# RetNet attention into a SwiGLU FFN on one core: second weight chunk and first unit's norm and product moved to earlier places

## The chip, the cores and the metric

The kernel runs on one core of one Trainium2 chip. The metric is device time in microseconds (us), from the first to the last instruction of the core, as the median of several executions. The engines are named as in the profile: PE (TensorE, matrix products) with PEld (its weight loads), DVE (VectorE), ACT (ScalarE), POOL (GpSimd) and SP (SyncE, which issues most of the transfers).

## The reference

Eight batches with eight heads of 576 rows by 64: retention (causal attention with a decay for each head in place of a softmax), then an RMS norm and a SwiGLU feed-forward over 4608 rows of 512.

```python
scores = scale * np.matmul(q, k.transpose(0, 1, 3, 2))
ret = scores * Dmat[None]                  # gamma_h ** (i - j) below the diagonal, else 0
attn = np.matmul(ret, v)                   # -> x: (4608, 512)

rms = np.sqrt(np.mean(x * x, axis=-1, keepdims=True) + 1e-06)
xn = x / rms * rms_g
g = xn @ w_gate                            # 512 x 1536
silu = g * (1.0 / (1.0 + np.exp(-g)))
val = xn @ w_val                           # 512 x 1536
out = silu * val @ w_out                   # 1536 x 512
```

q, k and v are float32. The three weight matrices arrive as float64 and must be rounded to float32 on the chip.

## The kernel before

The work is cut in two ways. Attention goes by *jobs*: a pair of heads of one batch. Jobs 0 to 3 are batch 0; jobs 4 to 7 are the first third of batch 1. The feed-forward goes by *units* of 384 rows: unit 0 needs jobs 0 to 3, unit 1 also jobs 4 to 7. This start, in which jobs 0 to 7 run while the first weights are loaded and rounded, is what the change edits. From unit 2 on, the kernel follows a regular pattern that stays as it is.

A job's q and k are turned (transposed) on PE with ACT copying the result out of PSUM, then `slot(j)` does the products of job j and the second half of job j - 1:

```python
def slot(j, rest=True):
    if rest and j > 0:
        values(j - 1)      # PE: av <- ret, v; then a memset of "tick" on POOL behind its last product
    if j < len(jobs):
        scores(j)          # PE: s <- qT, kT
        states(j)          # PE: s <- v, k
    if j < len(jobs):
        weigh(j)           # DVE: ret
    if j < 2 * NHP:
        sums(j)            # DVE: running state
    if rest and j > 0:
        carried(j - 1)     # PE: av <- qT, sum, waits for tick; then DVE: x <- av * gq (L435)
    ...
```

The norm of a unit is in four steps: `square` on ACT and `gather` on DVE (L487), `norm_1` (PE: mean square `ms`, L499; DVE: `r`, L504; POOL: POW, L505), `diagonals` on DVE (L547), and `norm_2` (PE: broadcast `rb`, L562; DVE: four scalings of x, L564).

The products of the first two units are made by a generator that yields after each. Half 0 of a matrix comes before half 1:

```python
def up_plain(u, m, g):
    if not (m or g):
        h_of[u] = ...
    for half in range(2):
        for i in (2 * g, 2 * g + 1):
            ps = bank(f"up_{u}_{m}_{half}_{i}")
            for c in range(NHP):
                nc.tensor.matmul(
                    ps[:, :U], lhsT=w_up[m][:, 4 * half + c, i * P : i * P + P],
                    rhs=x_of[u][:, c], start=(c == 0), stop=(c == NHP - 1),
                )
            h = h_of[u][:, half * NH + i]
            if m:
                nc.vector.tensor_tensor(out=h, in0=h, in1=ps[:, :U], op=ALU.mult)
            else:
                nc.scalar.activation(out=h, in_=ps[:, :U], func=AF.Silu)
            yield
```

The float64 weights come in chunks of 1024 KB. Chunk 0 is half 0 of the first columns of w_gate, chunk 1 is half 1, chunks 2 and 3 are the same of w_val. A chunk's words are read in integer and float steps, each one step of the generator `rounding`; `weights(n)` takes n steps:

```python
exponent(i)   # DVE L874: shift and mask; queues three Relus (L890) that act() gives to ACT later
yield
# mantissa(i):
#   DVE L901: mask; yield
#   DVE L906: add of the low word; yield
#   act(chunk=i): Relus still queued; DVE L911: sign; the room of the words is free
load_chunks(i + 5 if i else 0, nc.sync)
yield
# where chunk i + 1 is loaded: exponent(i + 1); yield
join(i)       # DVE L919: mantissa * exponent -> the float32 weights
yield
```

The start itself, before the change:

```python
load_chunks(1)
...
weights(3)
for j in range(2 * NHP):
    load_first(j, {0: range(2), 1: range(2, H)}.get(j))
    ...
    load_chunks((1, 1, 1, 1, 2, 2, 2, 3)[j], nc.sync)
...
turn(0)
scale_v(0)
act(3)
squares = []
...
for j in range(2 * NHP):
    slot(j)
    if j + 1 < 2 * NHP:
        turn(j + 1)
    if squares:
        gather(*squares.pop())
    for i in ((1,), (2,), (3,), (4, 5), (6,), (7,), (), ())[j]:
        scale_v(i)
    if j:
        u, c = divmod(j - 1, NHP)
        squares.append((u, c, square(u, c)))
    act(1)
    if j == 5:
        norm_1(0)
    elif j == 6:
        norm_2(0)
    weights((2, 0, 0, 1, 1, 1, 1, 0)[j])
    if j == 4:
        gather(*squares.pop())
    elif j == 5:
        diagonals(0)
    act(1)
gather(*squares.pop())
...
now = 0
for m, g in [(m, g) for g in range(NG) for m in range(2)]:
    for u in range(2):
        weights_to(4 * g + 2 * m + 1)
        for i, _ in enumerate(up_plain(u, m, g)):
            later(now)       # jobs 8 to 11 and their loads, at fixed counts
            now += 1
            if not (u or m or g):
                if i == 0:
                    values(2 * NHP - 1)
                    carried(2 * NHP - 1)
                    gather(1, NHP - 1, square(1, NHP - 1))
                elif i == 1:
                    norm_1(1)
                elif i == 2:
                    diagonals(1)
                elif i == 3:
                    norm_2(1)
            weights(2)
            act(1)
            if u and m and g == NG - 1:
                weights_to(len(chunks))
                next(made, None)     # combinations of w_out's blocks, DVE L690
            if i == 1:
                weights_to(4 * g + 2 * m + 2)
```

The order of instructions on each engine is that of the program. After this loop come the products across for units 1 and 0 (L726), which need differences of h (DVE, L710).

Of the kernel before, what the change touches and what calls it, by code (L numbers as in the profile page):

```python
# [41 lines left out]
def kernel(  # L42
# [11 lines left out]
    nc = tc.nc  # L54
# [242 lines left out]
    def scores(j):  # L297


        d = st[j]  # L300
        _, _, c0, c1 = jobs[j]
        s = d["s"] = trio.tile([P, 3, 512], F32, tag="s", name=f"s_{j}")
        for c in range(c0 // 2 * 2, (c1 + 1) // 2 * 2):
            i, odd = divmod(c, 2)
            c = min(max(c, c0), c1 - 1)
            for e in range(2):
                nc.tensor.matmul(  # L307
                    s[side(odd), e, i * L : i * L + L], lhsT=d["kT"][side(e), c * L : c * L + L],
                    rhs=d["qT"][side(e), c * L : c * L + L], start=True, stop=True,
                )  # L310
# [131 lines left out]
    def slot(j, rest=True):  # L442

        if j > len(jobs):
            return
        if rest and j > 0:
            values(j - 1)
        if j < len(jobs):
            scores(j)
            states(j)  # L450
        if j < len(jobs):
            weigh(j)
        if j < 2 * NHP:
            sums(j)
        if rest and j > 0:
            carried(j - 1)
        if 2 * NHP <= j < len(jobs):
            sums(j)
# [36 lines left out]
    def norm_1(u):  # L495

        ms = bank(f"ms_{u}")
        for s in range(NS):
            nc.tensor.matmul(  # L499
                ms[:, s : s + 1], lhsT=t_of[u][:, s * P : s * P + P], rhs=mean_w,  # L500
                start=True, stop=True,
            )
        r = tmp.tile([P, NS], F32, tag="r", name=f"r_{u}", bufs=1)
        nc.vector.tensor_scalar(out=r, in0=ms[:, :NS], scalar1=EPS, scalar2=None, op0=ALU.add)  # L504
        nc.gpsimd.tensor_tensor(out=r, in0=r, in1=mhalf.to_broadcast([P, NS]), op=ALU.pow)  # L505
        t_of[u] = r
# [45 lines left out]
    def norm_2(u):  # L552

        x = x_of[u]
        g = rms_k
        rb = t_of[u]
        if u < 3:
            g = rms_g  # L560
            rb = bank(f"rb_{u}")[:, :U]
            nc.tensor.matmul(rb, lhsT=ones, rhs=t_of[u], start=True, stop=True)  # L562
        for c in range(NHP):
            nc.vector.scalar_tensor_tensor(  # L564
                out=x[:, c], in0=x[:, c], scalar=g[:, c : c + 1], in1=rb,
                op0=ALU.mult, op1=ALU.mult,
            )
        if u < 2:
            return
        b11, b12 = x[:, :2, :HU], x[:, :2, HU:]  # L570
        b21, b22 = x[:, 2:, :HU], x[:, 2:, HU:]
        t = ffn.tile([P, 3, 2, HU], F32, tag="sums", name=f"sums_{u}")
        t2, t3, t4 = (t[:, i] for i in range(3))
        for o, a, b in ((t3, b22, b12), (b12, b12, b11), (t2, b22, b12), (t4, b21, t2)):
            nc.vector.tensor_tensor(out=o, in0=a, in1=b, op=ALU.subtract)

        t_of[u] = b11, b21, b12, t4, t2, t3, b22
# [282 lines left out]
    def load_chunks(n, queue=nc.scalar):  # L860

        nonlocal n_loads
        while n_loads < min(n, len(chunks)) and waits_at.get(spare(n_loads)) is None:
            load_chunk(n_loads, queue)
            n_loads += 1
# [96 lines left out]
    def weights(n):  # L962

        for _ in range(n):
            next(steps, None)
# [11 lines left out]
    def start():  # L977

        nonlocal now
        h_of[0] = ffn.tile([P, NF, U], F32, tag="h", name="h_0")  # L980
        tables = list(zip((causal, gv, gc, gq, gx), (_causal_table(), *_decay_tables(H, D))))

        def table(i, queue):
            t, values_ = tables[i]
            src = nc.inline_tensor(values_, name=t.tensor.name + "_table")
            queue.dma_start(out=t, in_=src.ap())

        make_identity(nc, ident)
        nc.scalar.activation(out=tick, in_=mhalf[:1], func=AF.Silu)
        nc.vector.memset(ones, 1.0)  # L990
        warm = bank("warm")
        for _ in range(6):
            nc.tensor.matmul(warm[:, :P], lhsT=ones, rhs=ones, start=True, stop=True)
        first_places.update(find_places())
        load_chunks(1)
        for i in (1, 0, 2):
            table(i, nc.scalar)
        weights(3)
        for j in range(2 * NHP):
            load_first(j, {0: range(2), 1: range(2, H)}.get(j))  # L1000
            if j == 1:
                table(3, nc.sync)
            load_chunks((1, 1, 1, 1, 2, 2, 2, 3)[j], nc.sync)
        table(4, nc.sync)
        nc.sync.dma_start(out=rms_g, in_=moe_rms_g.rearrange("(c p) -> p c", p=P))
        load_chunks(4, nc.sync)
        turn(0)
        scale_v(0)
        act(3)
        squares = []  # L1010

        def later(step):

            for i, at in enumerate((LATER_AT[0] - 9,) + LATER_AT[:-2]):
                if step == at + 2:
                    prepare_next(2 * NHP - 1 + i)
                elif step == at + 3:
                    load_next(2 * NHP - 1 + i)
            if step in LATER_AT:
                j = 2 * NHP + LATER_AT.index(step)  # L1020
                if j < LATER_JOBS:
                    slot(j, rest=(j > 2 * NHP))
                else:
                    values(j - 1)
                    carried(j - 1)

        for j in range(2 * NHP):
            slot(j)
            if j + 1 < 2 * NHP:
                turn(j + 1)  # L1030
            if squares:
# [4 lines that stand above are left out]
                u, c = divmod(j - 1, NHP)  # L1036
                squares.append((u, c, square(u, c)))
            act(1)
            if j == 5:
                norm_1(0)  # L1040
            elif j == 6:
                norm_2(0)
            weights((2, 0, 0, 1, 1, 1, 1, 0)[j])
            if j == 4:
                gather(*squares.pop())
            elif j == 5:
# [3 lines that stand above are left out]
        load_qk(2 * NHP)  # L1050
        load_kv(2 * NHP)
        made = combine_out()
        now = 0
        for m, g in [(m, g) for g in range(NG) for m in range(2)]:
            for u in range(2):
                weights_to(4 * g + 2 * m + 1)
                for i, _ in enumerate(up_plain(u, m, g)):
                    later(now)
                    now += 1
                    if not (u or m or g):  # L1060
                        if i == 0:
                            values(2 * NHP - 1)
                            carried(2 * NHP - 1)
                            gather(1, NHP - 1, square(1, NHP - 1))
                        elif i == 1:
                            norm_1(1)
                        elif i == 2:
                            diagonals(1)
                        elif i == 3:
                            norm_2(1)  # L1070
# [4 lines that stand above are left out]
                        next(made, None)  # L1075
                    if i == 1:
                        weights_to(4 * g + 2 * m + 2)
        for _ in made:
            pass
        for blk, t in first_blocks.items():  # L1080
            keep(blk, t)
        rest = across(1)
        next(rest)
        following(LATER_JOBS - 1)
        for i, _ in enumerate(rest):
            if i == 1:
                norm_0(2)
                differences(0)
            elif i == 2:
                norm_1(2)  # L1090
                diagonals(2)
            elif i == 4:
                norm_2(2)
        rest = across(0)
        next(rest)
        combine(1)
        slot(LATER_JOBS, rest=False)
        following(LATER_JOBS)
        for _ in rest:
            pass  # L1100
        combine(0)
        slot(LATER_JOBS + 1)
        load_next(LATER_JOBS + 1)
        turns.append(LATER_JOBS + 1)
# [74 lines left out]
```

## Time and profile before

| what | value |
|---|---|
| median of 3 runs | 1136.8 us (1135.39 to 1137.64) |
| profiled execution, span | 1135.3 us |
| PE busy | 1116.6 us (98%) |
| DVE busy | 732.7 us (65%) |
| mean granted clock of TensorE | 0.994 |
| first product of unit 1 (`up`, L652) starts at | 63.94 us |
| largest wait of PE between 20 and 66 us | 2.5 us, at L241 |

How to read it: the page gives the busy time of each engine over the whole span and in 40 equal slices, one digit of tenths to a slice; PEclk is the clock that TensorE was granted. In a line of a timeline stand the start, the length, the engine, the line of the program, the operation, out<-in by the names of the program, the shape and the count; in brackets, how long the engine had been idle before it and what released it. The waits list, for one engine, the total, the number and the longest.

### The profile page before, as it was taken

Reading aid. Unit: us, or ns where it says so; the run is one execution under the profiler, and the core shown is the slowest. Engines: PE = TensorE matmul, PEld = TensorE weight load, DVE = VectorE, ACT = ScalarE, POOL = GpSimd, SP = SyncE. Lnnn points to the kernel's source line nnn. Section 1 sums busy time; section 2 is a strip of 40 time slices with the busy share of each in tenths; the row PEclk is TensorE's granted clock in tenths of the full one; section 3 lists DMA queues with packets and bytes.
Section 4 is the critical chain, followed back from the end, with each engine's and each line's share of the span. In section 5 each row is a group of like instructions: output and inputs, shape, how many; then the busy total and the mean of one; then the engine's idle time right before and its main releaser. Section 6 shows DMA issues by size and latency. Waiting matters only on the chain.

```text
span 1135.3 us, 24783 instructions
## 1 busy us (share of the span) xinstructions
PE 1116.6 (98%) x10454; PEld 1042.3 (92%) x10454; DVE 732.7 (65%) x1452; ACT 258.6 (23%) x508; POOL 40.9 (4%) x68
## 2 busy tenths in 40 slices
PE   7899999999999999999999999999999999999998
PEld 6655567999999999999999999999999999999998
DVE  5788989655775784485677585465676666446352
ACT  5465551011212211211211121121120210120110
POOL 0000000460000000000000000000000000000000
PEclk9899999999999999999999999999999999999999
DMA  8744568336364374063553555315436503303304
GB/s 193 232 134 148 133 156 241 62 64 154 74 141 110 99 168 136 1 129 81 118 127 50 135 145 103 114 51 103 130 75 138 154 7 98 126 1 100 123 1 112
DMA packets 307040, 126.73 MB, mean 112 GB/s; under 512 B 284528, under 2 KB 289904, under 8 KB 306928
## 3 DMA queue, kind: packets, MB, share of 16 engines
q1 hardware_dynamic: 302640, 123.66, 43.2%
q8 instruction: 82, 1.34, 0.5%
q10 hardware_dynamic: 4288, 1.48, 0.5%
q14 instruction: 30, 0.25, 0.1%
HBM read 110.14 MB, written 14.94 MB: 110 GB/s over the span
## 4 chain that ended last, share of the span: by engine, by line
PE 96%; DVE 1%; DMA 1%; issue 1%; ACT 1%; SPq 0%; POOL 0%; POOLq 0%; ACTq 0%
PE x L595 14%; PE w L595 14%; PE z L595 14%; PE up L652 11%; PE xo L726 8%; PE wo L726 8%; PE zo L726 8%; PE y L595 7%; PE yo L726 4%; PE av L390 2%; PE av L412 2%; PE s L307 2%; PE s L329 1%; PE ms L513 1%; DMA first_sums<-in_v_dram 0%
## 5 line engine op out<-in xcount | busy, mean ns | idle before, releaser
L619 ACT COPY m<-x 128x384 f32<-128x384 f32 x60 | 28.7, 479 | 338.1 <-PE x L595 326.8
L726 PE MATMUL xo<-h,w_out 128*128 128x192 f32 x528 | 90.3, 328 | 0.0
L595 PE MATMUL w<-sums,w_val 128*128 128x192 f32 x480 | 88.6, 328 | 0.3
L595 PE MATMUL x<-x,w_gate 128*128 128x192 f32 x480 | 88.8, 328 | 0.0
L595 PE MATMUL x<-x,w_val 128*128 128x192 f32 x480 | 88.8, 328 | 0.0
L595 PE MATMUL w<-sums,w_gate 128*128 128x192 f32 x480 | 87.9, 326 | 0.0
L595 PE MATMUL z<-x,w_gate 128*128 128x192 f32 x480 | 87.8, 326 | 0.0
L595 PE MATMUL z<-x,w_val 128*128 128x192 f32 x480 | 87.8, 326 | 0.0
L726 PEld LDWEIGHTS xo<-h,w_out 128*128 128x128 f32 x528 | 85.9, 190 | 0.6
L726 PE MATMUL wo<-h,w_out 128*128 128x192 f32 x504 | 85.6, 326 | 0.4 <-DVE c_last L774 0.4
L602 DVE TENSOR_TENSOR u<-m,y 128x384 f32<-128x384 f32 x60 | 33.1, 552 | 79.1 <-PE y L595 79.1
L726 PEld LDWEIGHTS wo<-h,w_out 128*128 128x128 f32 x504 | 82.5, 190 | 0.7 <-DVE c_last L774 0.7
L595 PEld LDWEIGHTS w<-sums,w_val 128*128 128x128 f32 x480 | 79.2, 190 | 2.7 <-DVE c L602 2.7
L595 PEld LDWEIGHTS x<-x,w_gate 128*128 128x128 f32 x480 | 79.2, 190 | 0.8 <-issue 0.3
L595 PEld LDWEIGHTS x<-x,w_val 128*128 128x128 f32 x480 | 79.2, 190 | 0.6
L595 PEld LDWEIGHTS z<-x,w_gate 128*128 128x128 f32 x480 | 79.7, 190 | 0.0
L595 PEld LDWEIGHTS z<-x,w_val 128*128 128x128 f32 x480 | 79.7, 190 | 0.0
L595 PEld LDWEIGHTS w<-sums,w_gate 128*128 128x128 f32 x480 | 79.5, 190 | 0.1
L602 DVE TENSOR_TENSOR h<-u,w 128x384 f32<-128x384 f32 x60 | 33.0, 550 | 69.4 <-PE w L595 69.4
L614 ACT ACTIVATE h<-h 128x384 f32<-128x384 f32 x90 | 47.0, 523 | 88.6 <-DVE h L602 88.6
L652 PE MATMUL up<-x,w_gate 128*128 128x384 f32 x192 | 63.8, 489 | 1.7 <-DVE r L504 1.0
L652 PE MATMUL up<-x,w_val 128*128 128x384 f32 x192 | 63.2, 488 | 0.0
(189 smaller groups left out, 1778.0 us busy)
## 6 DMA issues: line engine op xcount, KB each, us to landing
w_out<-w_blocks SPq DMA_DIRECT2D x70, 768.0 KB, 5.0
out_dram<-o SPq DMA_DIRECT2D x364, 24.0 KB, 1.6
qraw<-in_q_dram SPq DMA_DIRECT2D x96, 72.0 KB, 2.6
kraw<-in_k_dram SPq DMA_DIRECT2D x96, 72.0 KB, 2.6
k<-in_k_dram SPq DMA_DIRECT2D x48, 128.0 KB, 2.9
v<-in_v_dram SPq DMA_DIRECT2D x48, 128.0 KB, 3.0
w_out<-in_moe_w_gate_dram SPq DMA_DIRECT2D x5, 1024.0 KB, 5.4
w_out<-in_moe_w_val_dram SPq DMA_DIRECT2D x3, 1024.0 KB, 5.3
```

The source lines that it names most:

```text
L307: nc.tensor.matmul(s[side(odd), e, i * L : i * L + L], lhsT=d["kT"][side(e), c * L : c * L + L], rhs=d["qT"][side(e), c * L : c * L + L], ...
L329: nc.tensor.matmul(o[side(e)], lhsT=d["k"][side(odd), i, e], rhs=d["v"][side(odd), i, e], start=True, stop=True,)
L390: mm = nc.tensor.matmul(av[odd][column(j, odd, e), i * L : i * L + L], lhsT=d["v"][side(odd), i, e] if c < NC - 1 else d["vt"][:, e], rhs= ...
L412: mm = nc.tensor.matmul(av[odd][column(j, odd, e), i * L : i * L + L], lhsT=d["sum"][c - 1][side(e)], rhs=d["qT"][side(e), c * L : c * L + L],
L513: nc.tensor.matmul(s, lhsT=ones, rhs=y, start=True, stop=True)
L595: nc.tensor.matmul(ps[:, i * HU : i * HU + HU], lhsT=w_up[m][:, 2 * blk + c, cut], rhs=t_of[u][blk][:, c], start=(start and i == c == 0), ...
L602: nc.vector.tensor_tensor(out=o, in0=a, in1=pairs_of(ps), op=ALU.add)
L614: nc.scalar.activation(out=o, in_=c, func=AF.Silu)
L619: nc.scalar.copy(out=s1, in_=pairs_of(x_))
L652: nc.tensor.matmul(ps[:, :U], lhsT=w_up[m][:, 4 * half + c, i * P : i * P + P], rhs=x_of[u][:, c], start=(c == 0), stop=(c == NHP - 1),)
L726: nc.tensor.matmul(ps[:, i * HU : i * HU + HU], lhsT=a[:, c, i * P : i * P + P], rhs=rhs[:, c], start=(start and i == c == 0), stop=False, ...
```

## The change

Four things are moved; no operation is added or taken away.

1. The load of chunk 1 is issued after job 3's loads instead of after job 4's.
2. The steps of its rounding move: one step in job 2, two in job 3, one in job 4, and in job 5 the exponent of chunk 2. The join of chunk 1 stays behind the loop over the jobs.
3. `norm_1(0)` and `norm_2(0)` go ahead of the turns of the next job, so that PE meets them before the transposes.
4. The first product of unit 0 is made in job 6, ahead of slot 7. The generator is created early and resumed later, so the loop over products counts one less: the second product is i = 1 of the first round, job 7's values come after it, and `norm_1(1)` comes after the third product.

What it is for: to give PE work in the waits of the start, and to have the weights and the norm ready sooner.

```diff
-            load_chunks((1, 1, 1, 1, 2, 2, 2, 3)[j], nc.sync)
+            load_chunks((1, 1, 1, 2, 2, 2, 2, 3)[j], nc.sync)
...
         squares = []
+        first = up_plain(0, 0, 0)
...
             slot(j)
+            if j == 5:
+                norm_1(0)
+            elif j == 6:
+                norm_2(0)
             if j + 1 < 2 * NHP:
                 turn(j + 1)
...
             act(1)
-            if j == 5:
-                norm_1(0)
-            elif j == 6:
-                norm_2(0)
-            weights((2, 0, 0, 1, 1, 1, 1, 0)[j])
+            if j == 6:
+                next(first)
+            weights((2, 0, 1, 2, 1, 1, 0, 0)[j])
...
                 weights_to(4 * g + 2 * m + 1)
-                for i, _ in enumerate(up_plain(u, m, g)):
+                whole = u or m or g
+                for i, _ in enumerate(up_plain(u, m, g) if whole else first, 0 if whole else 1):
                     later(now)
                     now += 1
                     if not (u or m or g):
-                        if i == 0:
+                        if i == 1:
                             values(2 * NHP - 1)
                             carried(2 * NHP - 1)
                             gather(1, NHP - 1, square(1, NHP - 1))
-                        elif i == 1:
+                        elif i == 2:
                             norm_1(1)
-                        elif i == 2:
                             diagonals(1)
                         elif i == 3:
                             norm_2(1)
```

## The prediction

> **What bounds the kernel now.** I read the page first, then the chain of waits, then the timelines of the engines up to 70 us. The page:
>
> ```profile
> PE 1116.6 (98%) x10454; PEld 1042.3 (92%) x10454; DVE 732.7 (65%) x1452; ACT 258.6 (23%) x508; POOL 40.9 (4%) x68
> ...
> PE   7899999999999999999999999999999999999998
> PEclk9899999999999999999999999999999999999999
> ```
>
> TensorE (PE) is the bound: after the first two of 40 slices (28 us each) every slice but the last is 9. The change edits the first 65 us, so its worth is how much earlier or later PE enters the saturated part. Everything after follows rigidly. The marker is the first product of unit 1, at 63.94 us before. The waits of PE up to 66 us say what can be won:
>
> ```profile
> PE turn_k L241 <- issue: 2.5, 1, 2.5
> ...
> PE av L390 <- ACT qT L252: 1.2, 2, 0.8
> PE up L652 <- DVE r L504: 1.0, 1, 1.0
> ...
> PE av L412 <- POOL tick L401: 0.8, 2, 0.5
> PE up L652 <- DVE x L564: 0.7, 1, 0.7
> ```
>
> Columns: total us, times, longest. After job 4's transposes begin, the waits are 2.5 (nothing visible released it), 0.8, 0.5, 0.3, 1.0 and 0.7. They sum to 5.8 us, 0.5% of the time: no outcome can leave the 2% band. The timeline of PE at the end of this part:
>
> ```profile
> 51.63 0.45 PE L390 MATMUL av<-ret,h 64*64 64x64 f32 x12
> 52.35 0.45 PE L412 MATMUL av<-qT,sum 64*64 64x64 f32 x8 [0.28 <-POOL tick L401]
> 52.73 2.85 PE L652 MATMUL up<-x,w_gate 128*128 128x384 f32 x8
> 55.41 0.77 PE L499 MATMUL ms<-mean_w,sq 128*128 128x1 f32 x6
> 57.19 5.40 PE L652 MATMUL up<-x,w_gate 128*128 128x384 f32 x16 [1.00 <-DVE r L504]
> 62.42 0.81 PE L562 MATMUL rb<-diag,ones 128*128 128x384 f32 x2
> 63.94 10.59 PE L652 MATMUL up<-x,w_gate 128*128 128x384 f32 x32 [0.71 <-DVE x L564]
> ```
>
> And VectorE (DVE) in the same stretch:
>
> ```profile
> 53.74 0.41 DVE L435 TENSOR_TENSOR x<-av,gq 128x128 f32<-128x128 f32 x2
> 54.74 0.56 DVE L487 TENSOR_TENSOR sq<-sq,sq 128x384 f32<-128x384 f32 x1 [0.59 <-ACT sq L477]
> 55.22 0.68 DVE L874 TENSOR_SCALAR w_gate<-w_out 128x1024 uint32<-128x1024 uint32 x1
> 55.82 1.22 DVE L919 SCALAR_TENSOR_TENSOR w_gate<-w_gate 128x1024 f32<-128x1024 f32 x1
> 56.96 0.15 DVE L504 TENSOR_SCALAR r<-ms 128x3 f32<-128x3 f32 x1
> ```
>
> The 1.0 us at 57.19 is put down to r, but the third product (half 1 of w_gate) needs chunk 1, whose last step is the join at L919, done at 57.04. That join stands in VectorE's program behind job 7's x (L435), the square on ScalarE and the gather (L487).
>
> **What the Trainium skill says.** "TensorE: Matmul & The Clock Gate", Architectural detail: ScalarE and VectorE are strict FIFO, only TensorE reorders, and only weight loads. The trace agrees: the join waits its turn although its inputs were ready long before (sign step at 49.96). Same page, Part 1: the clock is gated by activity in a free-running window of about 3.4 us, half rate after an idle one. The stretches show the granted clock at 0.50 from 33.9 to 37.2 (after the 2.5 us wait) and from 44.2 to 47.4, 1.00 between. "Runtime: NRT & Kernel Launch", Instruction fetch mechanics: instructions come in 16 KiB blocks of 256, the next fetched by a DMA while the current one runs. The page counts 82 packets and 1.34 MB on q8, 16 KB each. The DMA view has one of them starting at 31.0 us, the 2.5 us wait ends at 33.65 between two transposes without a semaphore between them: an instruction fetch, late because chunk 1 (1024 KB, issued 25.73, landed 5.4 us later) lay on the same DMA engines. "DMA: Bandwidth & Descriptors", Queues, rings and completion order: an engine takes a whole packet of one ring before it switches, which fits a delayed and not a blocked fetch.
>
> **The change, part by part** (times in the old kernel's clock; the phase before 22 us doesn't change).
>
> *Chunk 1's load* is issued near 22.1 instead of 25.73. Its contention moves from the fetch at 31.0 to the one that started at 24.36. In the three gaps before, a fetch was usable about 1.5 us after its packet's end (32.11 to 33.65). If the earlier one starts 2 us later, at 26.4, it ends at 27.3 and is usable at 28.8; PE crosses to that block at 27.93, so it waits about 0.9 us there. The next block is asked for then, and needs about 1.3 + 1.0 + 1.5 = 3.8 us uncongested against some 3 us of work in the block: 0.8 more. So 1.7 in place of 2.5 us: **minus 0.8**. But job 3 now has two Relus at its end (2 x 1.15 us on ScalarE) ahead of job 5's copies, and these would then arrive about when they do now: I keep **minus 0.4** of it.
>
> *Rounding sooner.* Exponent, mask and add of chunk 1 (0.68 + 0.68 + 1.22 us) go to jobs 2 and 3, where VectorE waited 1.19 and 1.86 us: mostly hidden. The sign step (1.22) goes to job 4, ahead of the last gather of unit 0, which ends near 40.9 instead of 40.84: nothing. In job 5 the copies of qT no longer queue behind Relus: they waited until 42.37, which was the 0.8 us wait.
>
> *Norm of unit 0 ahead of the turns.* The mean-square product now stands before job 6's turn and needs the gather at 40.9; the old order ran the turn at 40.36. So PE waits 0.5 there, does the ms (0.5) and the turn (1.0), the copies end at 43.0 and job 5's values start at 43.05 instead of 42.78. carried(5) still waits for the POW on GpSimd (44.2), as before: 44.45 against 44.35, **plus 0.1**. The broadcast product runs at 45.1 to 46.35 (half clock), the normalised x is ready from 47.1 to 48.7 instead of 48.4 to 50.0, beside job 7's turn on PE (to 47.9).
>
> *First product ahead of slot 7.* up0 47.9 to 50.5 without the 0.2 it loses now, slot 7 to 51.65, then up1 to 54.25, then values(7) and carried(7) with the tick wait of 0.3: done at 55.4. In the old kernel carried(7) is done at 52.8 with up1 (2.65) still to come: the same work, level to 0.1.
>
> *What follows is the cost.* In the new order nothing stands on PE between carried(7) and the third product, and the join stays behind carried(7) in VectorE's order: x 0.41, square 0.52, gather 0.56, join 1.22 and some 0.2 of hand-overs make 2.9 us. The third product starts near 58.3 instead of 57.19: **plus 1.1**. The ms product of unit 1 (0.55) moves behind it: **plus 0.5**. Its r then comes at 61.6, the POW (1.29) and the diagonals end at 63.8, and now chunk 2's mask and add (0.68 + 1.22) stand between the diagonals and the scaling of x: that starts at 65.6, and unit 1's first product at 66.25, where the old wait would have given 65.4: **plus 0.8**. Without the fetch's minus 0.4 the marker is 66.25 against 63.94, plus 2.3.
>
> *Half clock.* PE idles about 3 us before 58.3. If the window takes that for idle, 3.4 us at half rate follow, of which up to 2.8 hold products: a loss of 1.4 us, at about even odds as the phase is free: **plus 0.7**.
>
> *The end of the first two units.* The count of steps now starts one product later, so job 11's values come after the last up product. VectorE then has x (1.1 us) in front of the last combination (1.75) and the differences (1.35) that the second product across needs. Before, these end at 189.98 and the product starts at 190.19: a slack of 0.2. I get x from 186.4, the differences' end near 190.6: **plus 0.4**.
>
> Sum: 2.3 - 0.4 + 0.7 + 0.4 = 3.0 us. 1136.8 + 3.0 = 1139.8; I shade it to **1139.5** for the gain below.
>
> **Rivals.** (a) The change does what it is for: PE's small waits are filled, and the fetch, freed of chunk 1, comes in time. Then 2.5 us and the half clock after it (1.4) go, and the time could be 1135 or 1134 if the join were not in the way. For it: the fetch is the largest wait. Against: the join's place in VectorE's order, certain from the program. (b) The fetch only moves: all of the 2.5 us stays, now at 27.9, and the half clock with it: 1140. (c) DMA collision: chunk 5 is no longer held until 51.2 but goes at about 40.5, next to chunks 2, 3 and 4, and delays the fetch that started at 43.4. In the new order that block is needed near 50 (48.08 before), so I expect nothing; if it does bite, plus 1 to 2 and 1141. (d) No change to be measured, if gains and costs cancel: 1137.
>
> **Range and chances.** The old runs span 2.2 us. Rival (a) in part gives 1136, everything bad together 1142.8. I take 1136.0 to 1142.8. 2% is 22.7 us, out of reach of all of these: 98% within, 1% each side.
>
> **What would show it.** Right: a wait of 2 to 3 us of PE for VectorE (L919) ahead of the third product, near 55.4 to 58.3; the ms of unit 1 after it; the first product of unit 1 waiting over 1 us for L564, and starting 1.5 to 4 us later than 63.94; up0 near 48 without gaps; a shorter wait at turn_k, with a new one near 28; a short wait of zo for L710 near 190. Wrong: the join before 56, no fetch wait at all, or the marker before 63.9; then the time would be under 1136.

## The result, and the profile after

| | median | range | ratio to before, 95% interval |
|---|---|---|---|
| before | 1136.15 us | 1135.39 to 1137.64 | |
| after | 1147.88 us | 1147.03 to 1149.74 | 1.0104 [1.0086, 1.0121] |

The change makes the kernel 11.7 us slower. The prediction had the sign and one of the causes, but 1139.5 us and a range to 1142.8. The two profiled executions differ by 12.7 us in their spans (1148.0 and 1135.3). The page of the kernel after, of the same two rows as before:

```profile
PE   7889998999999999999999999999999999999998
PEclk9899999999999999999999999999999999999999
```

A slice is 28.7 us. The third (57 to 86 us) and the seventh (172 to 201 us) have an 8 where they had a 9: most of the time is lost in two places, at the start and late in the first two units. The waits of PE from 20 to 260 us (total us, times, longest) name them:

```profile
PE up L652 <- DVE h L658: 3.2, 1, 3.2
PE up L652 <- DVE w_gate L919: 2.9, 1, 2.9
PE ms L499 <- DVE sq L487: 2.0, 1, 2.0
PE av L390 <- issue: 1.2, 1, 1.2
PE up L652 <- DVE x L564: 1.0, 1, 1.0
...
PE turn_k L241 <- issue: 0.6, 1, 0.6
```

Three waits are new. The wait that the prediction took for an instruction fetch (an inference, as no releaser is shown), 2.5 us before, is now 1.2 and 0.6. Where the new ones stand at the start, in the timeline of PE after:

```profile
41.74 1.41 PE L499 MATMUL ms<-mean_w,sq 128*128 128x1 f32 x6 [2.05 <-DVE sq L487]
...
50.20 3.50 PE L652 MATMUL up<-x,w_gate 128*128 128x384 f32 x8
...
54.73 2.85 PE L652 MATMUL up<-x,w_gate 128*128 128x384 f32 x8
...
58.23 0.45 PE L412 MATMUL av<-qT,sum 64*64 64x64 f32 x8 [0.28 <-POOL tick L401]
61.58 4.51 PE L652 MATMUL up<-x,w_gate 128*128 128x384 f32 x8 [2.90 <-DVE w_gate L919]
...
70.94 10.59 PE L652 MATMUL up<-x,w_gate 128*128 128x384 f32 x32 [0.95 <-DVE x L564]
```

The three lines of `up` with 8 records are the first, second and third product (the fourth, at 66.52, is left out), and 70.94 is the marker, the first product of unit 1: 63.94 before, so 7.0 us are lost here. Of these equal products the second takes 2.85 us, the first 3.50 and the third 4.51. The difference is the clock. Stretches of the kernel after (length; busy time of PE, PEld, DVE, ACT, POOL with counts; granted clock; DMA share; GB/s):

```profile
37.90:41.30 3.40, 1.61 (x48) 1.22 (x47) 3.33 (x11) 1.74 (x6) 0.09 (x1) 1.00 0.87 263
41.40:51.50 10.10, 9.71 (x78) 6.58 (x79) 6.76 (x24) 4.27 (x10) 1.32 (x2) 0.50 0.79 296
...
61.90:65.10 3.20, 3.20 (x6) 1.66 (x5) 0.26 (x1) 1.15 (x1) 0.00 (x0) 0.50 0.06 14
...
184.70:188.00 3.30, 3.30 (x7) 1.79 (x6) 3.21 (x9) 0.68 (x2) 0.00 (x0) 0.50 0.88 224
```

The third figure from the right is the granted clock, 1.00 for full speed. Behind each of the three new waits the clock is at half: 10.2 us behind the first, 3.4 behind each of the others. The kernel before had 3.4 us of half clock twice in the same part, at 33.9 and 44.1.

Most of the rest is lost late, from the marker to the first product across (`xo`): 126.9 us after (70.94 to 197.85), 122.35 before (63.94 to 186.29), so 4.6 us more; 1.1 us come behind `xo`. In the kernel after:

```profile
184.21 12.28 PE L652 MATMUL up<-x,w_val 128*128 128x384 f32 x32 [3.19 <-DVE h L658]
...
197.85 4.17 PE L726 MATMUL xo<-w_val,w_out 128*128 128x192 f32 x24
```

The wait of 3.2 us, and 12.28 us for 32 records that take 10.59 at full clock (1.7 more), account for the 4.6 us. SyncE in that part, before and then after:

```profile
160.69 1.60 SPq L229 DMA_DIRECT2D vt<-in_v_dram  x1
162.39 0.54 SPq L857 DMA_DIRECT2D w_gate<-in_moe_w_out_dram  x1
165.99 1.95 SPq L156 DMA_DIRECT2D qraw<-in_q_dram  x4
```

```profile
159.90 0.61 SPq L229 DMA_DIRECT2D vt<-in_v_dram  x1
167.78 0.38 SPq L857 DMA_DIRECT2D w_gate<-in_moe_w_out_dram  x1
168.20 2.22 SPq L156 DMA_DIRECT2D qraw<-in_q_dram  x4
...
176.92 0.61 SPq L229 DMA_DIRECT2D vt<-in_v_dram  x1
```

In the kernel before, the loads of job 11 (from 154.52 us, ending with the vt at 160.69) stand ahead of the last weight chunk's load (162.39). In the kernel after, that load stands ahead of job 11's. It needs the room of an earlier chunk, which is free when the sign step ends at 167.76 us; so SyncE stands from 160.5 to 167.8 and the loads of job 11 behind it come some 7 us too late. ScalarE and VectorE then:

```profile
178.51 0.46 ACT L285 ACTIVATE v<-v,gv 128x192 f32<-128x192 f32 x1 [3.38 <-DMA v<-in_v_dram]
...
182.47 1.23 DVE L911 SCALAR_TENSOR_TENSOR w_gate<-w_gate 128x1024 uint32<-128x1024 uint32 x1 [3.94 <-ACT w_gate L890]
183.61 0.55 DVE L658 TENSOR_TENSOR h<-h,up 128x384 f32<-128x384 f32 x1
```

ScalarE has to scale job 11's v, which waits 3.4 us for the transfer, and the Relus (L890) stand behind it; the sign step (L911) waits for the Relus, the multiply of h (L658) stands behind the sign step, and PE waits for the multiply, as the room in PSUM is used up. So one late transfer is handed on through four queues, each of which works in order: SyncE, ScalarE, VectorE and PE.

### The profile page after: what moved, and what is told of

Its sections match the earlier page's. It is cut to its first block, busy times and chain, and to the rows that moved or that the text cites. A ratio compares the mean times of both kernels' runs of the same rounds, so it can differ in the third digit from the quotient of the medians.

```text
span 1148.0 us, 24782 instructions
## 1 busy us (share of the span) xinstructions
PE 1122.8 (98%) x10454; PEld 1045.1 (91%) x10454; DVE 733.3 (64%) x1452; ACT 258.4 (23%) x508; POOL 39.0 (3%) x68
## 4 chain that ended last, share of the span: by engine, by line
PE 91%; DVE 4%; SPq 1%; DMA 1%; ACT 1%; issue 1%; POOL 0%; DVEq 0%; POOLq 0%; ACTq 0%
PE w L595 13%; PE x L595 13%; PE z L595 13%; PE up L652 9%; PE xo L726 8%; PE wo L726 8%; PE zo L726 8%; PE y L595 6%; PE yo L726 4%; PE av L390 2%; PE s L307 1%; PE s L329 1%; PE av L412 1%; DVE sum L366 1%; DVE x L435 1%
## 5 line engine op out<-in xcount | busy, mean ns | idle before, releaser
L619 ACT COPY m<-x 128x384 f32<-128x384 f32 x60 | 28.7, 478 | 338.8 <-PE x L595 338.8
L652 PE MATMUL up<-x,w_gate 128*128 128x384 f32 x192 | 66.3, 503 | 3.9 <-DVE w_gate L919 2.9
L652 PE MATMUL up<-x,w_val 128*128 128x384 f32 x192 | 64.5, 497 | 3.2 <-DVE h L658 3.2
```

The costliest lines, as they stand in the source:

```text
L619: nc.scalar.copy(out=s1, in_=pairs_of(x_))
L652: nc.tensor.matmul(ps[:, :U], lhsT=w_up[m][:, 4 * half + c, i * P : i * P + P], rhs=x_of[u][:, c], start=(c == 0), stop=(c == NHP - 1),)
```

## The experiments

Each was timed beside the kernel before, which was at 1137.4 us (e1 to e4), 1136.8 (e5 to e8) and 1137.2 (e9 to e12); so ratios are compared. The start varies by up to 1.1 us between profiles, ahead of nearly all edited steps: job 3's turn begins at 24.1 us in e4, e10 and e12 and at 24.6 to 25.2 in all others. Markers are to be read with that, and the stretch from the marker to `xo` is compared everywhere. A profile shows one execution only: that of e1 took 1143.5 us, and its seven executions lie between 1138.5 and 1144.2.

**e1_count.** After, with the count aligned:

```diff
-        now = 0
+        now = 1
```

> The kernel after the change, but the count of products starts at 1, so that jobs 8 to 11 and their loads stand behind the same product as in the kernel before. Theory (order on SyncE): the late wait of PE, 3.2 us at 184 us for h L658 with a half-clock window behind it, comes from the last weight chunk's load standing ahead of job 10's loads on SyncE; with the order restored it goes, the zo wait too: about 5 us less than after, near 1142.5 us. Rival (the late wait follows from the start being 7 us late, so that rounding on VectorE lags): nothing changes there, near 1148 us. The start stays as in after: first product of unit 1 near 70.9 us on both.

Measured 1142.15 us, ratio 1.0039 [1.0023, 1.0055]. The late wait is gone, marker to xo takes 122.1 us (192.79 - 70.73), the zo product waits for nothing; the start is that of after, half clock from 40.9 to 51.1 and from 61.3 to 64.8. So 6 to 7 us are late (6.3 by the spans of the two profiles, 7.4 by the ratios, 1.0104 against 1.0039), and not a consequence of the start, which is as late as before this edit. (The loads held up are job 11's by the trace; the expectations here and below say job 10's.)

**e2_rounding.** Before, with the load and the rounding steps of the change alone:

```diff
-            load_chunks((1, 1, 1, 1, 2, 2, 2, 3)[j], nc.sync)
+            load_chunks((1, 1, 1, 2, 2, 2, 2, 3)[j], nc.sync)
...
-            weights((2, 0, 0, 1, 1, 1, 1, 0)[j])
+            weights((2, 0, 1, 2, 1, 1, 0, 0)[j])
```

> The kernel before with only the load of chunk 1 sooner and the rounding steps moved; norm and first product stay. Order on SyncE says: the last weight chunk's load stands ahead of job 10's loads here too (the steps are one further per product), so the late wait of 3 us and its half clock appear although the start is short: the time near 1140 us, plus 3 to 5. Rival (late wait follows from a late start): no late wait. For the start: if VectorE's longer program in jobs 3 and 4 is what made PE wait in after, a part of it shows here too, first product of unit 1 at 64 to 66 us; if the norm ahead of the turn is what exposes it, the marker is at 63 us or sooner, as the fetch wait gets shorter.

Measured 1140.92 us, ratio 1.0033 [1.0020, 1.0046]. The waits of PE from 90 us on:

```profile
PE up L652 <- DVE h L658: 3.1, 1, 3.1
```

The late wait is here with a start that isn't late at all: marker 63.69 us, then 125.3 to xo. The jobs keep their places in this kernel; what it shares with after is that the last weight load (157.94) stands ahead of job 11's loads (from 158.37), since the rounding is one step further. At the start the fetch wait is 0.9 in place of 2.5 us, and ms (1.0), ret (0.8) and a tick (1.1) take what this gives: sooner rounding is worth 0.25 us of the marker.

**e3_norm.** Before, with the norm's two parts of the change alone:

```diff
             slot(j)
+            if j == 5:
+                norm_1(0)
+            elif j == 6:
+                norm_2(0)
             if j + 1 < 2 * NHP:
                 turn(j + 1)
...
-            if j == 5:
-                norm_1(0)
-            elif j == 6:
-                norm_2(0)
```

> The kernel before with only the two parts of unit 0's norm ahead of the turns. Theory: the mean square then waits for the last gather of unit 0, which in the old rounding order ends near 40.8 us, so the wait is about 0.5 us and not 2.0; first product of unit 1 within 1 us of 63.9; time within 1.5 us of before. Rival (putting the norm ahead of the turn by itself exposes the gather and brings the run of half clock): a wait of 2 us at ms L499, half clock over two windows or more, plus 3 us or more. No late wait, as the order on SyncE is the old one.

Measured 1137.57 us, ratio 1.0001 [0.9992, 1.0011]: nothing. The wait at ms is 0.6 us, the marker 63.80. By itself the place of the norm is harmless.

**e4_first.** Before, with the hoisted first product alone (the edits of the change around `first`; load, rounding steps and norm as before):

```diff
+            if j == 6:
+                next(first)
             weights((2, 0, 0, 1, 1, 1, 1, 0)[j])
...
-                        if i == 0:
+                        if i == 1:
                             values(2 * NHP - 1)
```

> The kernel before with only the first product of unit 0 hoisted ahead of slot 7 (the norm's second part stays behind the turn); count as in the change. Theory (the join of chunk 1 stands behind job 7's gather and nothing stands on PE in between): a wait of 2.9 us for w_gate L919 ahead of the third product (3.5 with the exponent of chunk 2 in front of the join), often half clock behind it, so the first product of unit 1 comes 2.5 to 5 us later than 63.9; no late wait at 180 us, only 0.4 us more at zo: time 1139 to 1142 us. Rival (the wait for the join came from VectorE's longer rounding in jobs 2 to 4): no such wait, 1136 us.

Measured 1144.08 us, ratio 1.0063 [1.0046, 1.0079], more than I expected. The profiled execution, 1141.3 us, was the shortest of the six, so its trace explains only a part of this. Its marker is 67.26 us. The third product in its timeline:

```profile
57.53 5.12 PE L652 MATMUL up<-x,w_gate 128*128 128x384 f32 x8 [3.50 <-DVE w_gate L919]
```

The join's place alone makes 3.5 us, half clock follows from 55.4 to 62.2, and zo waits 0.4 us for L710: each as foreseen.

Marker to xo is 122.3: no late wait, though the jobs come one product later here. That too speaks for the order on SyncE and against the jobs' places as the cause of the late wait. e2, e3 and e4 together make 0.97%, the whole change 1.04%: nearly additive, within the intervals.

**e5_gather, e6_join, e7_both.** All on top of e1. e5:

```diff
+            if j == 4:
+                gather(*squares.pop())
             weights((2, 0, 1, 2, 1, 1, 0, 0)[j])
-            if j == 4:
-                gather(*squares.pop())
-            elif j == 5:
+            if j == 5:
                 diagonals(0)
```

> On top of e1_count: in job 4 the last gather of unit 0 goes ahead of the sign step of chunk 1. Theory (the 2.0 us wait at ms L499 is the sign step's 1.2 us in front of the gather, and the long half clock at 41 to 51 us follows from that wait): the gather ends near 40.4 us, the wait shrinks to 0.7 us, and the half clock to two windows or one, so the marker (first product of unit 1) is 1.2 to 3 us sooner than e1's 70.7. Rival (the half clock comes from light work on PE, transposes and small products, and not from the wait): the wait goes, the clock stays at half for three windows, and the marker is 1.2 us sooner or less. The 2.9 us wait for the join stays on both.

Measured 1142.01 us, ratio 1.0044 [1.0030, 1.0058]. The wait at ms goes from 2.05 to 1.1 us, the half clock at 41 us from three windows to two (40.6 to 47.4), the marker from 70.7 to 69.5. But behind the join the half clock now holds two windows (57.7 to 64.5), and the time is that of e1 within its interval. Inconclusive by itself.

e6:

```diff
-            weights((2, 0, 1, 2, 1, 1, 0, 0)[j])
+            weights((2, 0, 1, 2, 1, 1, 1, 0)[j])
```

> On top of e1_count: the join of chunk 1 is made in job 6, in VectorE's gap there, one step earlier than in the change. Theory (the third product waits for nothing but the join's place in VectorE's order): the 2.9 us wait for w_gate L919 goes without another in its place, and with it the half clock at 61 to 65 us, 3 to 4.5 us in all: marker near 66.5 to 67.5, time near 1138.5. Rival (another wait stands right behind it, the exponent or the bank): a wait of over 1 us ahead of the third product stays.

Measured 1139.41 us, ratio 1.0022 [1.0012, 1.0032]. The wait for L919 and the half clock behind it are gone, nothing stands in its place, the marker is 66.8. The wait for x L564 grows from 1.0 to 1.4. For this wait the join's place was the whole reason.

e7 has both edits:

> e5_gather and e6_join together, the change with its three faults of order mended. If the mechanisms add up: marker 63.5 to 66 us, time 1134.5 to 1137.5, within noise of the kernel before or 0.2% better. If the long half clock at 41 us stays, 1137 to 1139.

Measured 1138.14 us, ratio 1.0013 [1.0006, 1.0019], marker 64.6. With the three faults of order mended, some 1.4 us are left of 11.7, still not a gain. From e1 to e7 the marker comes 6.1 us sooner and the span of the profile shrinks by 5.2 us, but the ratios by 0.0026 only, 3.0 us: the executions confirm the direction, and about half of the size that the traces of the start show.

**e8_fill.** On top of e1, products that nobody reads (work is added, none left out):

```diff
+        def fill(n):
+            ps = bank(f"fill_{n}")
+            for _ in range(n):
+                nc.tensor.matmul(ps[:, :P], lhsT=ones, rhs=ones, start=True, stop=True)
...
             if j == 5:
+                fill(8)
                 norm_1(0)
...
                             gather(1, NHP - 1, square(1, NHP - 1))
+                            fill(12)
```

> On top of e1_count: products of ones by ones, whose result nobody reads, are added on PE ahead of the mean square of unit 0 (8 of 128x128) and ahead of the third product (12). They fill the two waits and add little to the path. If idling costs through the clock: the half clock at 61 to 65 us goes, and of the three windows at 41 to 51 us at least one, so the marker comes 1.5 to 4 us sooner than e1's 70.7 though work was added. Rival (half clock not set off by these waits): the same windows stay and the marker is level or up to 1 us later.

Stretches of e8, in the columns of above:

```profile
41.40:51.50 10.10, 9.51 (x132) 6.37 (x132) 7.24 (x25) 5.50 (x12) 1.35 (x3) 1.00 0.91 319
...
61.90:65.10 3.20, 3.20 (x12) 1.88 (x12) 1.93 (x6) 1.48 (x3) 0.85 (x1) 1.00 0.00 0
```

In this profile both stretches are at full clock, and so is everything from 32.1 us to the marker, which is at 66.4 instead of 70.7, with work added to the path. (The third product runs at 58.7 here, also at full clock. A half clock from 28.6 to 32.1, behind the fetch wait of 1.3 us, is one that e1 doesn't have.) So in this profile leaving PE without products was what set off the half clock, and the half clock cost 4.3 us, about as much as the two waits (2.05 and 2.90). The time, 1140.30 us, ratio 1.0036 [1.0023, 1.0050], isn't better than e1's by its interval, though. The waits of PE from 200 us on say where 3.2 us of the profile went:

```profile
PE av L412 <- issue: 1.9, 2, 1.3
PE x L595 <- issue: 1.7, 1, 1.7
```

In e1 these two are 0.2 and 0.2, so e8 has 3.2 us more. They are waits that nothing in the trace released, like the fetch wait of the start; 40 more matmul records and as many weight loads would shift all the block boundaries behind them. That they are fetches is my reading; it wasn't tried alone, and isn't shown.

**e12_order.** After, with one load moved by one step, the jobs where the change has them:

```diff
-                    load_chunks(i + 5 if i else 0, nc.sync)
+                    if i != 13:
+                        load_chunks(i + 5 if i else 0, nc.sync)
                     yield
+                    if i == 13:
+                        load_chunks(i + 5, nc.sync)
```

> The kernel after the change, in which only the load behind chunk 13's mantissa (the last weight load) is issued one step later, so that it stands behind job 10's loads on SyncE as in the kernel before; jobs 8 to 11 keep the places of the change. Order on SyncE says: the late wait of 3.2 us for h L658 and its half clock go, 5 to 7 us less than after, ratio to before near 1.004 to 1.005. Rival (the late wait comes from the jobs' places, one product later, and not from the load): the wait stays and the ratio is 1.010. The start stays as in after, marker near 70.9 us.

Measured 1144.53 us, ratio 1.0070 [1.0058, 1.0083]. The wait for h is 0.2 us in place of 3.2, and marker to xo is 122.5, against 122.35 in the kernel before: the order on SyncE was the cause of the late wait. It gives back 3.9 us by the ratios (1.0104 to 1.0070). A part of the 0.0031 (3.5 us) that keeps it above e1 is the other late cost, which the load had hidden in after:

```profile
198.04 2.22 PE L726 MATMUL zo<-t,w_gate 128*128 128x192 f32 x12 [1.76 <-DVE t L710]
```

It is the zo wait of the prediction, 1.8 instead of 0.4 us. The other half of the 3.5 us isn't explained by the trace.

**e9, e10, e11: towards a version that gains.** e9 is e2 with e5's gather edit and one step less in the first round:

```diff
-                    weights(2)
+                    weights(1 if now == 1 else 2)
```

> e2_rounding with two things mended: the gather ahead of the sign step in job 4, and one step less in the first round, so that the last weight load stands behind job 10's loads. If both faults of e2 are understood: no late wait, a wait of under 0.5 us at ms L499, marker 62.5 to 63.7 us, time 0 to 1.2 us under before (ratio 0.999 to 1.000).

Measured 1137.11 us, ratio 1.0003 [0.9995, 1.0012]. No late wait and none at ms; but the ret waits (1.3) and a tick (1.1) remain, the clock is at half for two windows (43.8 to 50.6), and the marker is 64.15, where I had 62.5 to 63.7. Level.

e10 is e7 with chunk 2's steps behind unit 1's scaling:

```diff
-                    weights(2)
+                    weights({3: 0, 4: 4}.get(now, 2))
```

> On top of e7_both: the steps of chunk 2 that stood between unit 1's diagonals and the scaling of x are taken after the scaling. Theory: the wait of 1.4 us for x L564 falls to 0.7 us, the marker comes 0.7 us sooner than e7's 64.6, ratio near 1.0005. Rival: the steps that are put off make a new wait later, and the ratio stays at 1.0013.

Measured 1137.49 us, ratio 1.0006 [0.9998, 1.0014], not to be told from e7's by the intervals. The wait for L564 is 0.7 us as foreseen, but the marker is only 0.4 us sooner than e7's, with a start 1.0 us sooner. The broadcast (rb L562) of unit 0 waits 1.0 us for the diagonals here, and the half clock lasts three windows (40.4 to 50.6). This lies ahead of the edit, so it is no effect of it; e11 shows where it comes from. e11 is e10 with the mean square behind the turn:

```diff
             slot(j)
-            if j == 5:
-                norm_1(0)
-            elif j == 6:
+            if j == 6:
                 norm_2(0)
...
             act(1)
+            if j == 5:
+                norm_1(0)
             if j == 6:
                 next(first)
```

> On top of e10: the mean square of unit 0 goes back behind job 6's turn, the broadcast stays ahead of job 7's. Theory: PE does the turn (1.0 us) while the gather ends, so the 1.1 us wait at ms L499 goes and the marker comes 0.5 to 1 us sooner than e10's; if the half clock at 42 to 49 us also shrinks to one window, 1.5 us sooner: ratio 0.9985 to 1.0. Rival: the POW on GpSimd comes later by the turn, carried(5) waits for it, and nothing is won.

Measured 1138.36 us, ratio 1.0012 [1.0005, 1.0019]: the ms wait goes, and the broadcast waits 1.8 us for the diagonals instead. The POW and VectorE in its trace:

```profile
42.62 0.86 POOL L505 TENSOR_TENSOR r<-r,mhalf 128x3 f32<-128x3 f32 x1 [4.83 <-DVE r L504]
```

```profile
44.73 0.69 DVE L874 TENSOR_SCALAR w_gate<-w_out 128x1024 uint32<-128x1024 uint32 x1 [2.19 <-DMA w_out<-in_moe_w_val_dram]
45.34 0.67 DVE L547 TENSOR_SCALAR diag<-ident,r 128x128 f32<-128x128 f32 x3
```

The POW is done at 43.5, but the diagonals stand behind chunk 2's exponent (L874), which waits 2.2 us for its load. In e10 the exponent waits 1.4 us in the same place, in e12 2.4 us (rb 0.9); in after and e7 the load was there. So it is once more the order of a queue, and the change itself put the exponent into job 5. Moving it behind the diagonals wasn't tried. No version beat the kernel before.

## Why the prediction was wrong

- **Bound and marker: right in part.** PE is the bound and a later marker goes with a longer time, but "everything after follows rigidly" is the sentence that failed: 4.6 us are lost between the marker and xo.
- **Chunk 1's load: right.** I had 0.9 + 0.8 us of fetch waits in place of 2.5; they are 1.2 and 0.6. PE comes to job 4's values 1.0 us sooner (37.76 against 38.71).
- **Rounding sooner, "mostly hidden": wrong.** With PE sooner, mask and add in job 3 are the chain: the add ends at 37.51 and job 4's ret starts there. The gather ends at 41.6; I had 40.9. From there the wait at ms is 2.05 us in place of the 0.5 I gave, as PE also comes 0.7 us sooner. e3 shows 0.6 without the longer rounding.
- **The norm ahead of the turns, "plus 0.1": wrong, through the clock.** I kept the old window of half clock, 44.1 to 47.5. The ms wait leaves PE busy for 1.6 of 3.4 us (the first stretch shown of after), and three windows at half rate follow. carried(7) ends at 58.7 instead of the 55.4 I had: 3.3 us, with the longer ms wait in it. e8 shows the part of the clock: with the wait filled, that run of half clock is gone.
- **The third product behind the join: right in cause and size.** I had 2.9 us from carried(7) to the product; after waits 2.90, e4 3.50, e6 none.
- **Half clock behind it, "plus 0.7 at even odds": under-sized.** It came in all five kernels whose third product waits for the join, in after, e1 and e12 for one window, in e4 and e5 for two. The third product takes 4.51 instead of 2.83: 1.7 us.
- **Scaling of x behind chunk 2's steps, "plus 0.8": over-sized.** The POW took 0.85 us where I had 1.29, and the wait is 0.95 instead of 0.71: plus 0.2.
- **End of the first two units, "plus 0.4": the step that failed worst.** I followed the shifted count to VectorE's last combination only. I didn't compare the order of loads on SyncE, where one step of rounding puts a blocked load ahead of job 11's. This makes the wait of 3.2 us with 1.7 us of half clock behind it, 4.6 us from marker to xo; taking the load out of the way alone gave back 3.9 us (e12), restoring the whole count 7.4 (e1). The zo wait that I did see is real, 0.4 us in e4 and 1.8 in e12, but in after the late load hides it.

The sum at the marker: my 2.3 - 0.4 + 0.7 = 2.6 against 7.0. The difference is the ms wait with its long half clock (3.3), the half clock behind the join (1.0) and small terms of both signs. What the 6 to 7 us of e1 hold beyond the 4.6 us up to xo isn't settled: the issue waits behind xo, 1.2 us in after and 0.4 in e1, are a part of it.

## What to carry to other kernels

When steps of a background task are advanced by one, print the order of every queue before and after, the one of the transfers first: a load that waits for room holds all loads behind it, here for 7.3 us. Work hoisted on the bound engine needs the next thing that this engine will ask for to be early as well; here the join in another queue stayed where it was and 2.9 us opened up. And count the clock that follows a wait of PE as part of its price: here 1.7 us each behind the waits of 2.9 and 3.2 us, and more behind the one of 2.05.

## What I had not expected of the hardware

Half clock lasted 10.2 us in one piece, three windows of 3.4 us, around and after a wait of 2.05 us (after, e1, e6 and e12 alike), though PE shows 9.71 of 10.10 us busy in it with transposes, small products and a part of one full product. The length of the wait doesn't settle it: e10 has the same 10.2 us with 1.1 us at ms and 1.0 at rb, e7 two windows after 1.1 us at ms, e2 one window (29.2 to 32.6) behind a fetch wait of 0.9 us, and e5 none behind an equal one. Nor does the busy share: the 3.4 us ahead of e10's half clock have PE busy for 2.28, while 1.82 of 3.4 in e1 (27.2 to 30.6) had no half clock behind them. In e8, 16 records of 128x128 products in the wait went with full clock through the same transposes. And adding 20 products at the start went with 3.6 us of waits without a releaser in the regular part, 2.4 us or more above those of every other kernel here.
